# Two layers of sliding attention and SiLU feed-forward on one Trainium2 core: the second layer's first feed-forward product by Strassen's scheme

## The chip, the cores and the metric

The kernel runs on one core of one Trainium2 chip. The metric is the device time of one execution in microseconds. Three runs of the kernel before took 2225.85, 2226.11 and 2229.71 us; the median is 2226.11 us.

## What is computed

Two layers with the same weights, each an attention over eight earlier positions two apart, and a feed-forward block; 2048 tokens of width D = 576, 32 heads, F = 4608.

```
x = x + attention(layernorm(x), wqkv, wo)     # 32 heads of 18, window 8, dilation 2, softmax
x = x + silu(layernorm(x) @ w1) @ w2          # w1 is 576 x 4608, w2 is 4608 x 576
x = x + attention(layernorm(x), wqkv, wo)
x = x + silu(layernorm(x) @ w1) @ w2
```

Inputs and output are float32. TensorE (PE) is fed float16: each operand is split into a high half and a low half (the rest after rounding), and a product is the sum of high x high, high x low and low x high.

## The kernel before

**Tiling.** The tokens go in four chunks of 512 (NJ = 4 blocks of 128), once per layer: stages s = 0 to 3 are the first layer, s = 4 to 7 the second; below they are called chunks 0 to 7. F is cut into 36 tiles of 128. Per chunk and tile f, `ffn` has 14 matmuls of 512 columns for the first product (L861, weights of w1 stationary, the chunk's normalised activations `xb` moving, into the PSUM bank `z`), a SiLU on ScalarE (L863, `hs` from `z`), the high half of h on ScalarE (L865) and its low half on VectorE (L868). The 14 passes cover K = 576 as four blocks of 128 with three passes each and a block of 64 that holds both halves. After a group of tiles (G1 = 9), the second product has, per token block j and tile, six matmuls of 288 columns (L882, h stationary, w2 moving, into `acc`), and VectorE adds the group's sum to x (L743). Chunk 0 makes the float16 halves of w1 and w2 (`raw_split`) and GpSimd (POOL) stores them in DRAM; later chunks load them back through SyncE's queue, 320 KB of w1 and 288 KB of w2 for a tile (`load_w1`, `load_w2`).

**Around it.** `front(s)` makes the chunk's inputs: layer norm, q, k, v (L566, 432 columns; for chunks 1 to 3 they are made ahead, in the first stage), the attention on VectorE (L664 to L705), the projection (L736) and the layer norm ahead of the feed-forward block. In the second layer `front(s+1)` runs on the other engines while PE is in chunk s. Operands are turned by DMA transposes on SyncE's queue (L361).

**What sets the order.** Every operation is a record with an engine, an assumed duration, a priority and the buffers it needs (`op`). `Plan.order` plays the program through with these durations and writes each engine's instructions in the order in which they would start; so each engine's order is fixed when the program is built, and an engine waits at an instruction whose inputs are late. A tag is a set of buffers of one kind (`z` has 2, `hs` 3, `h` 10, `w1` 6, `w2` 11); a buffer is taken when the first operation that needs it starts, and is free again after the last.

```
pp, pd = s + 0.5, s - 0.5          # PE of chunk s; its loads, SiLU and additions
op("PE", 3.05, mm, [(xT, j) for j in range(NJ)] + ka, [z], pp)
op("ACT", 0.7, ..., [z, ("s12", f)], [hs], pd, table="silu")
```

A front has priority s - 1.0, so on PE the q, k, v of chunk s + 1 go ahead of what is left of chunk s. Lower numbers go first.

Of the kernel before, what the change touches and what calls it, by code (L numbers as in the profile page):

```python
# [11 lines left out]
I32 = mybir.dt.int32  # L12
# [24 lines left out]
HSH = 2.0 ** -5  # L37

# [12 lines left out]
class Plan:  # L51
# [10 lines left out]
    def slots(self, tag, tiles, turns):  # L62

        self.tags[tag] = tiles
        self.turns[tag] = 0 if turns else None
        self.named[tag] = 0
# [35 lines left out]
    def order(self):  # L102
# [9 lines left out]
        times = [0.0]  # L112

# [53 lines left out]
        while done < len(self.ops):  # L167
# [9 lines left out]
            while events and events[0][0] <= now:  # L177
                _, _, b = heapq.heappop(events)
                free[b.tag].append(b.slot)
            for e in engines:  # L180
# [7 lines left out]
                while ready[e]:  # L188
# [5 lines left out]
                    if all(len(free[t]) - want.get(t, 0) >= c for t, c in n.items()) and all(  # L194
                            self.turns[b.tag] in (None, b.turn) for b in need):
                        o = x[2]
                        break
# [7 lines left out]
                for b in o.bufs:  # L205
                    if b.slot is None:
                        b.slot = free[b.tag].pop(0)
# [24 lines left out]
def sliding_attention_silu_ffn(ctx: ExitStack, tc: tile.TileContext, x, wqkv, wo, w1, w2, out):  # L232
# [17 lines left out]

    tag("x", 8, [P, D], F32)
    tag("xa", 1, [P, 9, TB], F16)
    tag("xb", 2, [P, 9, TB], F16)
    tag("wq", 2, [P, 10, 3 * UC], F16)
    tag("kv", 2, [P, NI, 2, UC], F32)
    tag("qt", 2, [P, NJ, UC], F32)
    tag("o", 1, [P, NJ, D], F32)
# [4 lines left out]
    tag("y", 2, [P, D], F32, turns=False)  # L262
    tag("yh", 2, [P, 9, P], F16, turns=False)
    tag("oT", 2, [P, 9, P], F16, turns=False)
    tag("wo", 1, [P, 10, D], F16)
    tag("w1", 6, [P, 10, P], F16)
    tag("w2", 11, [P, 2, D], F16)
    tag("h", 10, [P, 2, TB], F16)
    tag("hs", 3, [P, TB], F32)
# [3 lines left out]
    tag("z", 2, [P, TB], F32, ps)  # L273
    tag("acc", 2, [P, 2, 512], F32, ps, turns=False)
    tag("misc", 2, [P, 512], F32, ps, turns=False)
# [3 lines left out]
    w2s = [tc.dram_tile([P, 2 * D], F16, name=f"w2s{f}") for f in range(NFT)]  # L279
    wqs = [tc.dram_tile([P, 30 * UC], F16, name=f"wqs{u}") for u in range(NU)]  # L280
# [35 lines left out]
    shs = [cp.tile([P, NFT], F32, name=f"sh{i}") for i in range(2)]  # L316
    d2s = [cp.tile([P, NFT], F32, name=f"d2{i}") for i in range(2)]
    pace = cp.tile([1, 1], F32, name="pace")
    cg = cp.tile([P, NFT], F32, name="cg")
# [50 lines left out]
    def layer_norm(xs, prio, into, on_act, on_pe=False):  # L370
# [28 lines left out]
        def newton():  # L399
            v, r, a, b = (T(nt)[:, i, :] for i in (0, 1, 3, 4))  # L400
            if on_act == 2:
                nc.vector.tensor_scalar(v, T(st)[:, :, 0, 1], 1.0 / D, EPS, op0=ALU.mult, op1=ALU.add)
            else:
                nc.vector.tensor_scalar(v, T(mv)[:, :, 1], EPS, None, op0=ALU.add)
            nc.vector.tensor_scalar(a.bitcast(I32), v.bitcast(I32), 1, None, op0=ALU.logical_shift_right)
            nc.vector.tensor_scalar(r.bitcast(I32), a.bitcast(I32), -1, 0x5F3759DF, op0=ALU.mult, op1=ALU.add)
            for s in (1.0, LNS):

                nc.vector.tensor_tensor(a, r, r, op=ALU.mult)
                nc.vector.tensor_tensor(a, a, v, op=ALU.mult)  # L410
                nc.vector.tensor_scalar(b, a, 0.375 * s, -1.25 * s, op0=ALU.mult, op1=ALU.add)
                nc.vector.tensor_tensor(b, b, a, op=ALU.mult)
                nc.vector.scalar_tensor_tensor(r, b, 1.875 * s, r, op0=ALU.add, op1=ALU.mult)
            if on_act in (1, 3):
                nc.vector.tensor_scalar(T(nt)[:, 2, :], T(mv)[:, :, 0], -1.0, None, op0=ALU.mult)
        op("DVE", 2.4, newton, [(st, j) for j in range(NJ)] + [(mv, j) for j in range(NJ) if on_act != 2], [nt], prio)
        for j in range(NJ):
# [20 lines left out]
            else:  # L438
                op("DVE", 0.6, norm, [xs[j], (mv, j), nt], [y, (xT, "hold")], prio)
# [70 lines left out]
    def load_wq(u, prio):  # L510
        w = Unit("wq")
        op("SP", 0.4, lambda: nc.sync.dma_start(fl(T(w.bufs[0])), wqs[u]), [("wqs", u)], w.keys, prio, nbytes=P * 20 * QR)
        return w
# [83 lines left out]
    def attention(s, xT, wq, more=None):  # L597
# [4 lines left out]
        for u in range(NU):  # L602
# [11 lines left out]
            else:  # L614
# [13 lines left out]
                for j in range(NJ):  # L628
                    m = Buf("misc")

                    def evac(j=j, m=m, u=u, kv=kv, qt=qt):
# [5 lines left out]
                       [(xT, j)] + w.keys, [m], pr_)  # L637
# [113 lines left out]
    def load_w2(f, prio):  # L751
        w = Buf("w2")
# [24 lines left out]
    def raw_split(f0, prio):  # L777
# [11 lines left out]
        for f in fs:  # L789
# [6 lines left out]
        op("PE", 0.3, lambda: nc.tensor.matmul(T(m)[:, :2 * n], ones, fl(accw[:, sl, :]), start=True, stop=True),  # L796
           [("accw", f, i) for f in fs for i in range(2)], [m], prio - 1)
# [23 lines left out]
    def group_scale(i, g, n):  # L821

        sl = slice(g * n, (g + 1) * n)
# [7 lines left out]
        op("DVE", 0.7, fn, [("s12", f) for f in range(g * n, (g + 1) * n)], [("sh", i, g), ("cg", g)], -0.5)  # L831

    def ffn(s, xT, xs):
# [3 lines left out]
        lay, c = divmod(s, NC)  # L837
        for g in range(NFT // n):
            hb, wbs = [], []
            if raw:  # L840
# [5 lines left out]
                group_scale(0, g, n)  # L846
# [24 lines left out]
            for j in range(NJ):  # L871
# [3 lines left out]
                last = s == NL * NC - 1 and j == NJ - 1 and g == NFT // n - 1  # L875
                for hs_ in ((0,), (1,)) if last else ((0, 1),):
                    for t in range(0, n, step):
                        def mm2(j=j, acc=acc, t=t, step=step, hb=hb, wbs=wbs, hs_=hs_):
                            for q in range(t, t + step):
                                for m, (a, w) in enumerate(((0, 0), (0, 1), (1, 0))):  # L880
                                    for h in hs_:
                                        nc.tensor.matmul(T(acc)[:, h, 0:288], T(hb[q])[:, a, j * P:(j + 1) * P],  # L882
                                                         T(wbs[q][0])[:, w, h * 288:(h + 1) * 288],
                                                         start=q == 0 and m == 0, stop=q == n - 1 and m == 2)
                        op("PE", 0.37 * step * len(hs_), mm2, [(hb[q], a) for q in range(t, t + step) for a in range(2)]
                           + [k for q in range(t, t + step) for k in wbs[q][1]], [(acc, h) for h in hs_], pp)
                    if last:
                        h, = hs_

                        def add_half(j=j, acc=acc, g=g, h=h):  # L890
                            x_ = T(xs[j])[:, h * 288:(h + 1) * 288]
                            nc.vector.scalar_tensor_tensor(x_, T(acc)[:, h, 0:288], d2s[i][:, g:g + 1], x_,
                                                           op0=ALU.mult, op1=ALU.add)
                        op("DVE", 0.45, add_half, [(acc, h), ("sh", i, g), xs[j]], [(xs[j], h)], pd)
# [100 lines left out]
```

## Time and profile before

| | us |
|---|---|
| runs (three) | 2225.85, 2226.11, 2229.71 |
| profiled execution, first to last instruction | 2229.8 |
| PE busy | 2180.4 (98%) |
| VectorE (DVE) busy | 1393.3 (62%) |
| ScalarE (ACT) busy | 747.4 (34%) |
| POOL busy | 206.3 (9%) |

The profiled execution is one execution; its span is as long as the slowest of the three runs. In the profile's rows, PE is the matmul itself, PEld the load of its stationary operand; L861 is line 861. The row of a group gives its busy time, the mean of one instruction in ns, and the idle time ahead of it with what ended it. Matmuls are pipelined: the mean of one contains the filling of the pipe, so the pace of a run of them is read from the start of a run to the start of the next.

### The profile page before, as it was taken

Reading aid. Unit: us, or ns where it says so; the run is one execution under the profiler, and the core shown is the slowest. Engines: PE = TensorE matmul, PEld = TensorE weight load, DVE = VectorE, ACT = ScalarE, POOL = GpSimd, SP = SyncE. Lnnn points to the kernel's source line nnn. Section 1 sums busy time; section 2 is a strip of 40 time slices with the busy share of each in tenths; the row PEclk is TensorE's granted clock in tenths of the full one; section 3 lists DMA queues with packets and bytes.
Section 4 is the critical chain, followed back from the end, with each engine's and each line's share of the span. In section 5 each row is a group of like instructions: output and inputs, shape, how many; then the busy total and the mean of one; then the engine's idle time right before and its main releaser. Section 6 shows DMA issues by size and latency. Waiting matters only on the chain.

```text
span 2229.8 us, 33919 instructions
## 1 busy us (share of the span) xinstructions
PE 2180.4 (98%) x13858; PEld 1350.7 (61%) x13858; DVE 1393.3 (62%) x2047; ACT 747.4 (34%) x1211; POOL 206.3 (9%) x341
## 2 busy tenths in 40 slices
PE   5999999999999999999999999999999999999999
PEld 3556565656666666655666656666666566666665
DVE  7999989889988311359834597336971389511111
ACT  6455777543132122224212232222322223222222
POOL 2133555200001000000000000000000000000000
PEclk9999999999999999999999999999999999999999
DMA  5577667784645433455445454454453643433331
GB/s 152 165 206 274 235 224 240 200 231 155 184 152 154 116 103 105 150 128 178 116 112 160 103 176 121 125 159 131 135 132 120 167 140 117 91 115 123 112 113 40
DMA packets 220564, 332.18 MB, mean 149 GB/s; under 512 B 107240, under 2 KB 127572, under 8 KB 216440
## 3 DMA queue, kind: packets, MB, share of 16 engines
q1 hardware_dynamic: 191408, 230.47, 36.4%
q0 software_dynamic: 20704, 78.02, 10.3%
q10 hardware_dynamic: 8296, 21.52, 3.5%
q8 instruction: 108, 1.77, 0.3%
q14 instruction: 48, 0.39, 0.1%
HBM read 240.08 MB, written 47.03 MB: 129 GB/s over the span
## 4 chain that ended last, share of the span: by engine, by line
PE 85%; DVE 6%; DMA 4%; issue 2%; ACT 1%; POOL 1%; ACTq 0%; SPq 0%; DVEq 0%; POOLq 0%
PE z L861 36%; PE acc L882 34%; PE misc L566 7%; PE acc L736 4%; PE z L566 3%; DMA w<-in_B_w_dram 1%; DVE pr L664 1%; DMA kv<-kv 1%; DVE pr L697 1%; DVE lg L668 1%; DMA oT<-yh 1%; DMA h<-in_A_wqkv_dram 1%; DVE x L743 0%; DVE w L807 0%; DVE pr L704 0%
## 5 line engine op out<-in xcount | busy, mean ns | idle before, releaser
L861 PE MATMUL z<-xb,w 128*128 128x512 f16 x4032 | 882.8, 380 | 7.9 <-issue 3.9
L882 PE MATMUL acc<-w,h 128*128 128x288 f16 x6912 | 856.1, 286 | 2.2 <-DVE h L868 1.3
L882 PEld LDWEIGHTS <-h 128*128 128x128 f16 x6912 | 676.4, 98 | 179.9 <-DVE h L868 1.6
L861 PEld LDWEIGHTS <-w 128*128 128x128 f16 x4032 | 394.8, 98 | 475.7 <-issue 6.7
L863 ACT ACTIVATE hs<-z,d 128x512 f32<-128x512 f32 x288 | 197.6, 686 | 979.9 <-PE z L861 962.2
L868 DVE SCALAR_TENSOR_TENSOR h<-hs,sh,h 128x512 f16<-128x512 f32 x288 | 213.8, 748 | 311.7 <-ACT h L865 311.6
L743 DVE SCALAR_TENSOR_TENSOR x<-acc,d,x 128x576 f32<-128x576 f32 x135 | 109.9, 814 | 325.1 <-PE acc L882 325.0
L664 DVE TENSOR_TENSOR pr<-qt,kv 128x2304 f32<-128x2304 f32 x64 | 163.3, 2551 | 89.3 <-DMA kv<-kv 66.4
L865 ACT ACTIVATE h<-hs,sh 128x512 f16<-128x512 f32 x288 | 207.5, 721 | 9.4 <-DVE d L830 0.3
L566 PEld LDWEIGHTS <-xa 128*128 128x128 f16 x1344 | 131.7, 98 | 121.2 <-issue 7.1
L566 PE MATMUL misc<-wq,xa 128*128 128x432 f16 x1008 | 190.0, 349 | 3.8 <-ACT xa L359 2.5
L697 DVE TENSOR_TENSOR pr<-kv,pe 128x1152 f32<-128x1152 f32 x128 | 169.0, 1352 | 1.2
L668 DVE TENSOR_REDUCE lg<-pr 128x128 f32<-128x2304 f32 x64 | 163.1, 2548 | 1.2
L704 DVE TENSOR_TENSOR pr<-pr 128x1152 f32<-128x1152 f32 (+1 forms) x128 | 135.1, 1056 | 3.5
L736 PE MATMUL acc<-wo,oT 128*128 128x288 f16 x896 | 114.8, 288 | 4.6 <-DMA oT<-yh 4.6
L736 PEld LDWEIGHTS <-oT 128*128 128x128 f16 x896 | 88.3, 99 | 30.1 <-DMA oT<-yh 4.9
L633 ACT ACTIVATE kv<-misc,du 128x288 f32<-128x288 f32 x80 | 40.0, 500 | 138.5 <-PE misc L566 79.6
L906 POOL DMA_DIRECT2D out_dram<-x x12 | 6.5, 546 | 698.3 <-DVE x L743 698.3
L687 ACT ACTIVATE pe<-lg 128x256 f32<-128x256 f32 x32 | 13.3, 416 | 169.2 <-DVE lg L678 161.3
L566 PEld LDWEIGHTS <-xb 128*128 128x128 f16 x448 | 43.7, 98 | 38.6 <-ACT xb L359 0.9
L384 DVE BATCH_NORM_STATS2 st<-x 128x6 f32<-128x288 f32 x128 | 52.0, 448 | 10.9 <-DMA x<-in_A_x_dram 5.9
L743 DVE SCALAR_TENSOR_TENSOR x<-acc,so,x 128x576 f32<-128x576 f32 x32 | 26.1, 815 | 29.5 <-PE acc L736 29.4
(121 smaller groups left out, 1127.4 us busy)
## 6 DMA issues: line engine op xcount, KB each, us to landing
w<-w1s SPq DMA_DIRECT2D x252, 320.0 KB
w<-w2s SPq DMA_DIRECT2D x252, 288.0 KB
wq<-wqs SPq DMA_DIRECT2D x17, 1080.0 KB
kv<-kd POOLq DMA_DIRECT2D x8, 1584.0 KB, 8.2
w1s<-w POOLq DMA_DIRECT2D x36, 320.0 KB, 4.2
w<-in_B_w_dram POOLq DMA_DIRECT2D x36, 288.0 KB, 5.3
w2s<-w POOLq DMA_DIRECT2D x36, 288.0 KB, 4.2
kv<-kv ACTq DMA_DIRECT2D x20, 504.0 KB
```

Of the source, the lines that this page charges most:

```text
L566: nc.tensor.matmul(T(m)[:, :3 * UC], a, b, start=n == 0, stop=n == len(pl) - 1)
L664: nc.vector.tensor_tensor(T(pr), T(qt)[:, j:j + 2, None, :].to_broadcast([P, 2, W, UC]), win(T(kv), j, 2), op=ALU.mult)
L668: nc.vector.tensor_reduce(T(lg)[:, j:j + 2].rearrange("p a w h -> p (a w h)"), T(pr).rearrange("p a w (h d) -> p (a w h) d", d=DH), axis=A ...
L697: nc.vector.tensor_tensor(T(pr)[:, a].rearrange("p w (h d) -> p w h d", d=DH), v, T(pe)[:, j + a, :, :, None].to_broadcast([P, W, UH, DH]) ...
L704: nc.vector.tensor_tensor(t[:, :, 0:h, :], t[:, :, 0:h, :], t[:, :, h:2 * h, :], op=ALU.add)
L736: nc.tensor.matmul(T(acc)[:, h, 0:288], a, b[:, h * 288:(h + 1) * 288], start=n == 0, stop=n == len(pl) - 1)
L743: nc.vector.scalar_tensor_tensor(t, T(acc)[:, :, 0:288], d, t, op0=ALU.mult, op1=ALU.add)
L861: nc.tensor.matmul(T(z), v, u, start=m == 0, stop=m == len(pl) - 1)
L863: op("ACT", 0.7, lambda z=z, hs=hs, f=f: nc.scalar.activation(T(hs), T(z), AF.Silu, scale=d1[:, f:f + 1]), [z, ("s12", f)], [hs], pd, tabl ...
L865: op("ACT", 0.72, lambda hs=hs, h=h, f=f: nc.scalar.activation(T(h)[:, 0, :], T(hs), AF.Copy, scale=shs[i][:, f:f + 1]), [hs, ("sh", i, g) ...
L868: op("DVE", 0.75, lambda hs=hs, h=h, f=f: nc.vector.scalar_tensor_tensor(T(h)[:, 1, :], T(hs), shs[i][:, f:f + 1], T(h)[:, 0, :], op0=ALU. ...
L882: nc.tensor.matmul(T(acc)[:, h, 0:288], T(hb[q])[:, a, j * P:(j + 1) * P], T(wbs[q][0])[:, w, h * 288:(h + 1) * 288], start=q == 0 and m = ...
```

## The change

**Seven products for eight.** Two tiles of F make a pair (18 pairs, `NP`). The token blocks of a chunk are taken as two halves (blocks 0, 1 and blocks 2, 3), K = 576 as two halves of 288, and the pair's 256 columns as two tiles: a 2 x 2 by 2 x 2 block product, done with seven block products P1 to P7 in place of eight. Each block product has a weight form of 288 x 128 and an activation form of 288 x 256 (256 tokens). A form is stored in five blocks of 128 rows (`KB`): two high, one that holds both halves of the last 32 rows, two low; the product is seven matmuls of 256 columns.

```
def product(k, z, first, last, wf=wf):
    def mm():
        t, w, v = T(z)[:, 0:2 * P], T(wf[k]), T(xf[k])
        pl = ((0, 0), (3, 0), (0, 3), (1, 1), (4, 1), (1, 4), (2, 2))
        for m, (u, r) in enumerate(pl):
            nc.tensor.matmul(t, w[:, u, :], v[:, r, :], start=first and m == 0, stop=m == 6, skip_group_check=True)
    op("PE", 0.78, mm, [wf[k], (xf[k], 0), (xf[k], 1)], [z], pp)
```

In `ffn_pairs` the sums of the scheme are made partly in PSUM, partly in SBUF: products are added into three banks c, a, b, and between them a bank is copied out by ScalarE (`snap`, L1045) or added to a copy by VectorE (`add`, L1048).

```
product("P5", c, True, False)
product("P1", a, True, False)
snap(c, 3)
snap(a, 0)
product("P3", c, False, True)
product("P6", a, False, False)
product("P2", b, True, True)
snap(a, 1)
add(b, 0)
add(c, 1)
product("P7", a, False, False)
add(a, 3)
product("P4", a, False, True)
```

Then come three SiLUs on ScalarE (L1064, L1066, L1068), the high half of h for the pair (L1071, 1024 columns) and the low half (L1074 on VectorE). The second product (`second`, L1095) has the same matmuls as before; groups are 5, 4, 5 and 4 pairs (`G2`).

**Weight forms (`prepare`).** While the first layer runs, at priority `PREP` = 2.6, each pair's raw w1 is loaded once more by POOL (4 + 8 DMAs, L936 and L939), VectorE makes four sums (L947, 384 columns each), ScalarE the high halves (L955) and VectorE the low halves (L962) of seven forms, and POOL stores them (`wfs`, 1120 KB a pair, L967). The second layer loads a form of 160 KB for each product (`load_wf`, L972).

**Activation forms (`forms`).** In place of the second layer's layer norm into `xb`, VectorE normalises into `ya`, `yb` and makes eight differences; each of the seven forms is split by ScalarE and VectorE in two parts and turned by two DMA transposes.

**Buffers.** Many tags now share memory (`area`, `part`, and `places`, which the planner keeps apart): the weight forms lie in w1's place, the prepared forms in those of `wq` and `xa`, the activation forms (nine buffers `xf`, seven in use by a chunk) in that of `xb`, `ya` in that of the attention's output. In the second layer `z` and `misc` are four banks for products and for q, k, v alike, one buffer is left for a quarter of wqkv (`wz`), and the first layer norm of chunk 4 and these loads wait until the last pair's forms are stored:

```
+    def load_wq(u, prio, kind="wq"):
+        w = Unit(kind)
+        wait = [("wfs", NP - 1)] if kind == "wz" else []
...
-            o = attention(s, layer_norm(X[s], s - 1.0, "xa", False), lambda u: load_wq(u, s - 1.0))
+            o = attention(s, layer_norm(X[s], s - 1.0, "xa", False, late=[("wfs", NP - 1)]), lambda u: load_wq(u, s - 1.0, "wz"))
...
-        XT[s] = layer_norm(X[s], s - 1.0, "xb", s == 1, s == 0)
+        XT[s] = layer_norm(X[s], s - 1.0, "xb", s == 1, s == 0) if s < NC else forms(X[s], s - 1.0)
...
-        ffn(s, XT[s], X[s])
+        (ffn if s < NC else ffn_pairs)(s, XT[s], X[s])
+        if s == 0:
+            for q in range(NP):
+                prepare(q, PREP)
```

The scales of a pair's two tiles have to be equal, so the small matmul that sums squares in `raw_split` (18 calls) gets a second one that adds the neighbour's:

```
-        op("PE", 0.3, lambda: nc.tensor.matmul(T(m)[:, :2 * n], ones, fl(accw[:, sl, :]), start=True, stop=True),
...
+            nc.tensor.matmul(out, ones, v, start=True, stop=False)
+            nc.tensor.matmul(out, ones, turned, start=False, stop=True)
```

**How instructions stand, VectorE in chunk 4.** Before, in the feed-forward block of the second layer, while the next chunk's attention runs (L664, L668), VectorE's order has the low halves of h (L868) between the long operations:

```order
L868 SCALAR_TENSOR_TENSOR h4_118<-hs2_126,sh1_281,h4_118 128x512
L868 SCALAR_TENSOR_TENSOR h5_119<-hs1_125,sh1_281,h5_119 128x512
L664 TENSOR_TENSOR pr0_87<-qt0_81,kv0_79 128x2304
L868 SCALAR_TENSOR_TENSOR h6_120<-hs0_124,sh1_281,h6_120 128x512
L668 TENSOR_REDUCE lg0_84<-pr0_87 128x128
```

In the change the same place (pairs 11 to 13 of chunk 4; L744 and L748 are the attention's lines there) reads, with the banks z0, z1, misc0 and misc1:

```order
L1048 TENSOR_TENSOR wq_69<-z0_101,wq_69 128x256
L1048 TENSOR_TENSOR wq_69<-misc1_104,wq_69 128x256
L748 TENSOR_REDUCE lg0_86<-pr0_89 128x128
L1048 TENSOR_TENSOR wq_69<-misc0_103,wq_69 128x256
L1048 TENSOR_TENSOR hs_72<-misc1_104,hs_72 128x256
L1074 SCALAR_TENSOR_TENSOR h_71<-wq_69,sh2_268,h_71 128x1024
L1048 TENSOR_TENSOR hs_72<-z0_101,hs_72 128x256
L744 TENSOR_TENSOR pr0_89<-qt1_85,kv1_83 128x2304
L1048 TENSOR_TENSOR hs_72<-z1_102,hs_72 128x256
```

VectorE now reads PSUM banks that PE needs again, three times a pair, between the same long operations. On PE the products of these pairs stand so (one row of each product's seven matmuls; the bank tells the product: pair 12's P5, P1, then P2, P3, P6, then pair 11's last):

```order
L1041 MATMUL z0_101<-xb_67,w1_70 128x256
...
L1041 MATMUL z1_102<-xb_67,w1_70 128x256
...
L1041 MATMUL misc1_104<-xb_67,w1_70 128x256
...
L1041 MATMUL z0_101<-xb_67,w1_70 128x256
...
L1041 MATMUL z1_102<-xb_67,w1_70 128x256
...
L1041 MATMUL misc0_103<-xb_67,w1_70 128x256
```

Between two products into the same bank that need a copy in between, two others stand here (P1 and P2 between P5 and P3 in z0). Over the second layer's 343 waits of a product for ScalarE or VectorE, one product stands between in 14 cases; in the others there are at least two products, or a piece of twelve second-product matmuls.

**POOL in the first layer.** The weight forms' loads and stores stand alone in POOL's order from chunk 2 to the last quarter of chunk 3's first products; two pairs of them:

```order
L967 DMA wfs9_206<-xa_66 128x4480
L936 DMA wq_69<-in_B_w1_dram 128x2x128 x4
L939 DMA wq_69<-in_B_w1_dram 32x2x128 x8
L967 DMA wfs10_207<-xa_66 128x4480
L936 DMA wq_69<-in_B_w1_dram 128x2x128 x4
```

The store of a pair stands behind the twelve loads for the pair after next. ScalarE's high halves of a pair (L955) wait for the store of the pair before, as the forms have one buffer (`wg`); the loads wait for the pair's first low halves (L962). Between the store of pair 10 and that of pair 17 the program has 264 matmuls of 512 columns and 580 of 288 on PE.

**PE at the end of chunk 3.** Before, the projection for chunk 4 (L736) ends with 140 first-product matmuls (512 columns) and 432 second-product matmuls (288 columns) of chunk 3 still to come. In the change it ends here (L816), and behind it stand 28 and 216 of them; then come the first products of chunk 4:

```order
L816 MATMUL acc1_106<-wo0_93,yo_73 128x288
...
L1137 MATMUL z0_101<-xb_67,w1_70 128x512
...
L1156 MATMUL acc0_105<-w2_94,h_71 128x288
...
L1156 MATMUL acc1_106<-w2_94,h_71 128x288
...
L1041 MATMUL z0_101<-xb_67,w1_70 128x256
```

The front of chunk 4 has moved later against PE's work: its first q, k, v matmul stood behind 116 of the first layer's 144 tiles of the first product, and now stands behind 122.

More of the change, by code (lines that the diff above doesn't have):

```diff
@@ L37 @@
 HSH = 2.0 ** -5
+NP = NFT // 2
+KH = D // 2
+KB = 5 * P
+LNX = 512.0
+G2 = (5, 4, 5, 4)
+W2N = 11
+PREP = 2.6
 class Buf:
@@ L112, in order, with open_slots @@
         times = [0.0]
+        taken = {}
+        def open_slots(t):
+            return [i for i in free[t] if not any(
+                lo < b and a < hi for n, lo, hi in self.places[t][i] for a, b in taken.get(n, ()))]
         def arrive(o):
@@ L873, in ffn @@
                 step = n if n < 6 else 3
[L875 to L894, printed above, removed]
```

333 lines of the change are left out of this document (278 added, 55 removed).

## The prediction

> **What bounds the kernel now.** The page comes first: PE is busy 98% of the span, and the chain that ended last is 85% PE. So time is what PE's instructions take, unless a change makes PE wait.
>
> ```profile
> PE 2180.4 (98%) x13858; PEld 1350.7 (61%) x13858; DVE 1393.3 (62%) x2047; ACT 747.4 (34%) x1211; POOL 206.3 (9%) x341
> PE 85%; DVE 6%; DMA 4%; issue 2%; ACT 1%; POOL 1%; ACTq 0%; SPq 0%; DVEq 0%; POOLq 0%
> ```
>
> Next come the windows. The second row is one chunk of the second layer (chunk 4 into 5): columns are length, then busy time of PE, PEld, DVE, ACT, POOL, then clock, DMA share, GB/s.
>
> ```profile
> 300.00:350.00 50.00, 47.68 (x292) 28.34 (x291) 43.60 (x76) 36.54 (x68) 27.29 (x48) 1.00 0.66 224
> 1350.70:1620.35 269.65, 269.37 (x1707) 166.68 (x1705) 165.20 (x228) 71.90 (x114) 2.21 (x4) 1.00 0.48 137
> ```
>
> PE has 0.28 us idle in 269.65, so in the second layer there is no wait to remove: a gain can come only from fewer or shorter PE instructions. PE's timeline of that chunk gives their pace (start, length, instruction, count; a run's time goes to the next run's start).
>
> ```profile
> 1350.69 21.32 PE L861 MATMUL z<-xb,w 128*128 128x512 f16 x98
> 1371.84 7.02 PE L736 MATMUL acc<-wo,oT 128*128 128x288 f16 x56
> ...
> 1381.72 7.02 PE L736 MATMUL acc<-wo,oT 128*128 128x288 f16 x56
> 1388.58 3.18 PE L861 MATMUL z<-xb,w 128*128 128x512 f16 x14
> 1391.60 26.62 PE L882 MATMUL acc<-w,h 128*128 128x288 f16 x216
> 1418.06 27.36 PE L861 MATMUL z<-xb,w 128*128 128x512 f16 x126
> 1445.26 26.62 PE L882 MATMUL acc<-w,h 128*128 128x288 f16 x216
> 1471.72 24.34 PE L861 MATMUL z<-xb,w 128*128 128x512 f16 x112
> 1495.89 18.05 PE L566 MATMUL misc<-wq,xa 128*128 128x432 f16 x98
> 1513.78 3.19 PE L861 MATMUL z<-xb,w 128*128 128x512 f16 x14
> ...
> 38.01 0.67 PE L357 MATMUL acc<-ident,yh 128*128 128x128 f16 x9
> L357 PE MATMUL acc<-ident,yh x180: 216/219/314, 16.1 to 221.2; 128*128 128x128 f16 x180
> ```
>
> 512 columns: 27.20 / 126 = 0.2159 us. 432: 17.89 / 98 = 0.1825. 288: 26.46 / 216 = 0.1225. The last two rows are of chunk 0's transposes of 128 columns, each with a stationary load of its own: nine took 0.67 us, less the 0.219 that one lasts (the middle of the three durations), over 8, is 0.056 us. The four lie on a line, 0.417 ns a column and some 2.5 ns each, so 256 columns take 0.1092 us (an estimate).
>
> **The change: what it removes.** Per chunk of the second layer, 36 x 14 = 504 matmuls x 0.2159 = 108.8 us go, and 18 x 49 = 882 x 0.1092 = 96.3 us come. That is -12.5 us a chunk, **-50.0 us** for four. The bounds: at the pace of 288 columns the gain is 0.8 us a chunk, 3 in all (rival C); below 0.1092 nothing speaks for it. The second product keeps its matmuls.
>
> Added on PE: the second small matmul in `raw_split`, 18 times.
>
> ```profile
> 345.07 0.28 PE L796 MATMUL misc<-accw,ones 128*128 128x4 f32 x2
> 345.21 0.38 PE L861 MATMUL z<-xb,w 128*128 128x512 f16 x1
> ```
>
> The call that is there (two records) delays the next matmul by 0.14 us and lasts 0.28: +2.5 to +5 us; I take **+2.5**, the delay. Chunk 0's order of PE changes in places too; its idle time there (2.3 us in the first of the two windows) is at stake both ways, which I carry as 0 ± 5.
>
> **What it adds beside PE, and what of it PE waits for.** Products are half as long as a tile before (0.76 for 3.02 us), and PE now waits for copies out of its banks.
>
> ```profile
> L868 DVE SCALAR_TENSOR_TENSOR h<-hs,sh,h 128x512 f16<-128x512 f32 x288 | 213.8, 748 | 311.7 <-ACT h L865 311.6
> L664 DVE TENSOR_TENSOR pr<-qt,kv 128x2304 f32<-128x2304 f32 x64 | 163.3, 2551 | 89.3 <-DMA kv<-kv 66.4 <-ACT kv L633 21.9
> L865 ACT ACTIVATE h<-hs,sh 128x512 f16<-128x512 f32 x288 | 207.5, 721 | 9.4 <-DVE d L830 0.3
> L863 ACT ACTIVATE hs<-z,d 128x512 f32<-128x512 f32 x288 | 197.6, 686 | 979.9 <-PE z L861 962.2 <-DMA kv<-kv 10.8 <-DVE lg L668 5.5
> L805 ACT ACTIVATE w<-w,s 128x640 f16<-128x640 f32 x36 | 29.3, 818 | 11.9 <-PE z L861 10.8 <-DVE s L330 1.0
> L807 DVE SCALAR_TENSOR_TENSOR w<-w,s,w 128x640 f16<-128x640 f32 x36 | 31.4, 877 | 0.0
> L678 DVE TENSOR_TENSOR lg<-lg,mx 128x256 f32<-128x256 f32 x32 | 13.6, 425 | 1.1
> 1543.93 0.50 ACT L633 ACTIVATE kv<-misc,du 128x288 f32<-128x288 f32 x1 [10.34 <-DVE pr L697]
> 1544.33 0.38 ACT L635 ACTIVATE qt<-misc,du 128x144 f32<-128x144 f32 x1
> 1544.75 7.46 PE L566 MATMUL misc<-wq,xa 128*128 128x432 f16 x40 [0.28 <-ACT qt L635]
> 1547.50 0.50 ACT L633 ACTIVATE kv<-misc,du 128x288 f32<-128x288 f32 x1 [2.14 <-PE misc L566]
> ```
>
> Loads: a copy of 256 columns out of PSUM takes 0.47 us on ACT (between the 0.38 and 0.50 of 144 and 288), an addition 0.43 on DVE. For 1024 columns: ACT 0.721 + 512 x 0.76 ns (818 less 721 over 128) = 1.11; DVE 0.748 + 512 x 1.01 ns = 1.26. A pair then costs ACT 4 x 0.47 (three copies, one SiLU) + 0.69 + 0.42 + 1.11 = 4.1 us, before 2 x 1.41 = 2.8; DVE 3 x 0.43 + 1.26 = 2.5, before 1.5. Per chunk that is +23 us on ACT and +19 on DVE, and `forms` adds, by the same slopes, some 10 on ACT (14 parts) and 7 on DVE: ACT 106 and DVE 191 us of a chunk of 257. Neither is full; only the moments count.
>
> The shortest hand-over: the run at 1544.75 ends its first 14 matmuls at 1547.30 (14 x 0.1825), ACT starts at 1547.50, and after ACT's end at 1544.71 PE starts at 1544.75. So product, copy, next product costs 0.20 + 0.47 + 0.04 = 0.71 us, less than the one product of 0.76 that stands between in the tightest 14 places; elsewhere there is 1.47 or more. PE waits where a copy is queued behind something longer than planned: an addition (L1048) behind a 2.55 us attention operation comes 0.20 + 2.55 + 0.43 = 3.2 us after its product, 1.7 late against 1.5 of cover. There are 16 such operations in each of three chunks; the planner gave them 2.57 us and 0.45 to 0.48 to the copies, so its own places hold. Bounds 0 and 48 x 1.7 = 82 us; near the first, since no assumed duration is short: I take 3 late ones, **+5**.
>
> **The preparation** costs a pair on DVE four sums of 384 columns at 0.55 and low halves of 2688 columns in four operations, 2.72 + 4 x 0.23, together 5.8; on ACT 2.04 + 4 x 0.33 = 3.4; on POOL 13 DMAs. That is 105 us of DVE, 61 of ACT and 234 DMAs. It lies beside chunks 1 to 3, where DVE has time. But its chain may set PE's pace, since copies and low halves of chunk 3 are queued behind L955 and L962 on engines that keep their order.
>
> ```profile
> L770 POOL DMA_DIRECT2D w<-in_B_w_dram x36 | 27.5, 764 | 14.7 <-issue 6.2 <-DMA kd<-w 4.8 <-PE z L861 1.8
> L772 POOL DMA_DIRECT2D w<-in_B_w_dram x72 | 38.4, 537 | 5.5 <-DMA w<-in_B_w_dram 3.0 <-issue 1.3 <-PE z L861 1.1
> w<-in_B_w_dram POOLq DMA_DIRECT2D x36, 256.0 KB, 5.0
> wqs<-wq POOLq DMA_DIRECT2D x2, 1080.0 KB, 8.1
> wqs<-wo POOLq DMA_DIRECT2D x1, 1080.0 KB, 5.4
> wqs<-h POOLq DMA_DIRECT2D x5, 216.0 KB, 9.9
> ```
>
> A round of it: ACT's first high half 1.11, DVE's low half 1.26, twelve loads issued 4 x 0.54 to 0.76 + 8 x 0.54 = 6.5 to 7.4, the store's issue 0.54 and its landing 5.4 to 8.1 (1120 KB, nearest the 1080 KB rows): 14.8 to 18.4 us. PE's work between two stores is 264 x 0.2159 + 580 x 0.1225 = 128.0 over 7 = 18.3 us. So it holds, barely at the upper end. With a microsecond of queueing the upper end is 19.4, over by 1.1 x 12 late pairs = 13 us. Bounds 0 and 13, above that rival B; I take **+3**.
>
> **The ends of chunks.** Behind the projection for chunk 4 PE now has 28 x 0.2159 + 216 x 0.1225 = 32.5 us (before: 140 and 432 matmuls, 83 us).
>
> ```profile
> 1363.40 3.25 SPq L361 DMA_TRANSPOSE oT<-yh  x2
> ...
> 1375.46 4.70 SPq L361 DMA_TRANSPOSE oT<-yh  x2
> ...
> 1395.83 7.72 SPq L361 DMA_TRANSPOSE xb<-yh  x4
> ```
>
> From the projection's last matmul (1388.58) to the first transpose took 7.3 us. `forms` has three more normalisations and eight differences before it, some 5 us: 12; a copy and a low half add 1.3. A transpose of 1152 columns takes SyncE 1.6 us (3.25 / 2; the new ones have 640), and PE could use two that ended at 1380.16 from 1381.72. So the first form is there at 12 + 1.3 + 3.2 + 1.6 = 18 us, and the last of the seven, fourteen transposes on, at 37 at the latest, when PE after 32.5 us has six products ahead of it. Bounds 0 and 10; **+2**. At the three later ends, five of the seven forms wait for chunk s's last pair to free its buffers, under 192 x 0.1225 = 23.5 us of second product; ten transposes take at most 16 and the wait after them: 0 to 3 each, **+3** together. Loads of weight forms are 1120 KB a pair for 640 before, +8.8 MB or 34 GB/s in a chunk; with 137 x 269.65 / 257 = 144 that is 178 GB/s, under the 224 of the first window: 0.
>
> **Sum.** -50.0 + 2.5 + 5 + 3 + 2 + 3 = -34.5. The profiled execution, 2229.8 us, is as long as the slowest run, with nothing around its span; the median is 3.7 lower. 2229.8 - 34.5 - 3.7 = **2191.6**.
>
> **The rivals.**
> A: *copies bind.* If all of ACT's 106 us a chunk fell into the 96.3 us of products, PE would wait 9.7 a chunk, 39 for 5: 2226, no change. For it: one ACT order for copies, SiLU, q, k, v and halos. Against: a third of PE's chunk is second product, which the planner uses as filler. 0.07.
> B: *the preparation paces the first layer.* If each of the twelve loads waits for one issued eight earlier to land (5.0 us: 10 us a round) and the store lands in 9.9 as the wqs<-h row did, a round is 1.11 + 1.26 + 10 + 0.54 + 9.9 = 22.8, 4.5 over 18.3; x 17 = 77 in place of 3: 2266, **slower**. It decides from 18.3 + 37.5/17 = 20.5 us a round. For it: one buffer of forms. Against: the rows above. 0.10.
> C: *the stationary load shows.* If a 256-column matmul cannot hide the next load, it takes the 0.1225 of 288 columns: 47 us of the gain gone, 2238, slower. Against: 0.056 us at 128 columns with loads. 0.03.
> The Trainium skill ("TensorE: Matmul & The Clock Gate", Back-to-back issue gap) says that a stream of load and matmul pairs runs at about 81 ns with 128 columns against 56 for an isolated gap; by that, as an estimate, 256 columns would take 25 ns more, 118 us a chunk, and the kernel 2280. By that rule the change loses; the trace's 56 ns, with a load for each transpose, does not agree, and its chance is in C's.
>
> **How the numbers follow.** The forecast has 0.80; A 0.07, B 0.10, C 0.03. A measurement tells 0.2%, 4.5 us, from no change. Faster: 0.80 + 0.02 of A = 0.82; same: 0.04 of A; slower: B, C and 0.01 of A = 0.14. Range: low, all waits 0 and chunk 0 luckier by 5: 2229.8 - 50 + 2.5 - 5 - 3.7 = 2174. High: the waits at 18 (copies), 13, 8, the small matmul 5: -50 + 44 = -6, 2220, and a little of A: 2222. Outside are B, C, 0.05 of A and 0.02 below, 0.20 in all.
>
> **What would show it.** Right: L1041's 3528 matmuls at 0.109 us, a chunk of the second layer in about 259 us, PE's idle time there under 5 a chunk. For A: waits of PE for ACT and DVE (L1045, L1048) of ten or more a chunk. For B: the first layer from 560 to 1120 us longer, POOL or ACT's L955 waiting for the store. For C: PE's busy time in L1041 over 400 us. A wait at L646 in chunk 3 or a gap at the first L1041 would be the ends of chunks. Wrong would be above all a chain of the preparation that is longer than its rows.

## The result and the profile after

| | before | after |
|---|---|---|
| median of four runs, us | 2226.24 | 2207.53 |
| lowest to highest, us | 2225.85 to 2229.71 | 2206.12 to 2214.10 |
| profiled execution, span, us | 2229.8 | 2206.6 |

The ratio is 0.9917, 95% interval 0.9901 to 0.9933: faster by 18.7 us, where 34.5 were forecast. The gain is real, about half its size is missing, and the profile says where. The page of the changed kernel, its first line and its chain:

```profile
PE 2139.0 (97%) x15406; PEld 1503.4 (68%) x15406; DVE 1578.4 (72%) x2453; ACT 905.3 (41%) x1617; POOL 347.2 (16%) x575
PE 90%; DMA 5%; DVE 2%; ACT 1%; issue 1%; ACTq 0%; POOL 0%; SPq 0%; DVEq 0%; POOLq 0%
```

PE is still the bound, but its share fell from 98% to 97% while its work shrank. The windows of the changed kernel (columns as in the prediction) show where it idles:

```profile
560.00:790.00 230.00, 230.00 (x1538) 150.19 (x1536) 215.13 (x301) 77.92 (x103) 51.92 (x85) 1.00 0.63 189
790.00:1020.00 230.00, 230.00 (x1449) 141.45 (x1447) 109.98 (x180) 87.30 (x124) 68.70 (x118) 1.00 0.67 211
1250.00:1350.00 100.00, 94.39 (x672) 66.36 (x671) 70.62 (x70) 34.07 (x68) 5.81 (x8) 0.97 0.55 157
1610.00:1870.00 260.00, 252.66 (x2030) 198.93 (x2029) 181.40 (x283) 96.89 (x194) 2.16 (x4) 0.99 0.65 177
```

While the preparation runs (first and second row) PE has no idle time at all. In the second layer, where PE had 0.28 us idle in 269.65 before, it now misses 5.61 us in one stretch and 7.34 in another, and in both the granted clock is below 1. The waits of PE from 1120 us on, in full (engine, tile and line, what it waited for, total, times, longest):

```profile
PE z L1041 <- ACT hs L1045: 7.2, 1, 7.2
PE misc L1041 <- ACT hs L1064: 5.6, 1, 5.6
PE misc L1041 <- ACT wq L1045: 2.7, 1, 2.7
PE acc L1095 <- DVE x L1104: 0.6, 1, 0.6
```

Three waits, 15.5 us, all for ScalarE (two copies out of a bank, L1045, and a SiLU, L1064, that also reads a bank), one in each of chunks 4, 5 and 6. PE's timeline at the first, and at a quiet place (the first two rows of the fence):

```profile
1421.97 1.69 PE L1041 MATMUL z<-xb,w 128*128 128x256 f16 x14
1423.50 0.93 PE L1041 MATMUL misc<-xb,w 128*128 128x256 f16 x7
...
1309.21 1.63 PE L1095 MATMUL acc<-w,h 128*128 128x288 f16 x12
1316.46 1.65 PE L1041 MATMUL misc<-xb,w 128*128 128x256 f16 x7 [5.61 <-ACT hs L1064]
1317.90 1.70 PE L1041 MATMUL z<-xb,w 128*128 128x256 f16 x7
1319.39 1.35 PE L1041 MATMUL misc<-xb,w 128*128 128x256 f16 x7
1320.58 0.93 PE L1041 MATMUL z<-xb,w 128*128 128x256 f16 x7
```

The quiet place gives the pace: 1.53 / 14 = 0.1093 us for 256 columns, as forecast. After the wait seven matmuls take 1.44, 1.49 and 1.19 us instead of 0.76, until the clock is back, so the 5.61 us cost 7.4. ScalarE's timeline at the same place tells why the SiLU was late; the last three rows are an ordinary set of the same instruction, and the same place one and two chunks on:

```profile
1305.99 0.37 ACT L715 ACTIVATE qt<-misc,du 128x144 f32<-128x144 f32 x1
1306.12 9.77 ACTq L725 DMA_DIRECT2D kv<-kv  x4
1315.93 0.47 ACT L1064 ACTIVATE hs<-misc,accw 128x256 f32<-128x256 f32 x1 [9.57 <-DMA kv<-kv]
...
1279.38 2.89 ACTq L725 DMA_DIRECT2D kv<-kv  x4
...
1569.69 6.91 ACTq L725 DMA_DIRECT2D kv<-kv  x4
...
1824.38 10.55 ACTq L725 DMA_DIRECT2D kv<-kv  x4
```

L725 are the four halo DMAs of a unit (a quarter of the heads), issued from ScalarE's queue. Thirteen of the sixteen sets from 1000 us on take 2.87 to 3.46 us to issue, which is what the planner assumes (3.2). The third set that is issued while PE is in chunk 4, 5 and 6 (it belongs to the chunk after) takes 9.77, 6.91 and 10.55, and ScalarE's reading of the banks stands behind it. Before, the sixteen sets (L645) took 2.87 to 3.40; the one at the same place:

```profile
1280.93 3.10 ACTq L645 DMA_DIRECT2D kv<-kv  x4
```

SyncE's timeline in the changed kernel, same moment:

```profile
1305.58 0.32 SPq L592 DMA_DIRECT2D wq<-wqs  x1
1306.35 13.60 SPq L972 DMA_DIRECT2D w<-wfs  x7
```

SyncE begins a quarter of wqkv (1080 KB) and then seven weight forms. The single instructions of the trace give the semaphore that each DMA completes on (S, numbers of the trace; start in us):

```
SP   1305.58 wqkv quarter  S107      SP   1307.87 weight form 3  S105
ACT  1306.12 halo 1        S108      SP   1308.64 weight form 4  S106
SP   1306.35 weight form 1 S102      SP   1312.22 weight form 5  S107  (after the wqkv quarter landed)
ACT  1306.71 halo 2        S100      ACT  1315.07 halo 4         S108  (waits for S108: halo 1 landed)
SP   1307.11 weight form 2 S103      SP   1318.14 weight form 6  S100  (waits for S104, S100: halos 3 and 2)
ACT  1307.59 halo 3        S104
```

SyncE's and ScalarE's DMAs share eight semaphores (S100 and S102 to S108 in these traces; POOL's DMAs have S110 to S117), dealt out in the program's order; a DMA waits until the one that had its semaphore before has landed. With five weight forms dealt in between, halo 4 got halo 1's semaphore, and halo 1 took 8.9 us to land. The transfer was nearly as long before (7.9 us for halo 1 of the set at the same place); the wait for it is new. At the other two places the semaphore came from another DMA: in chunk 5 halo 4 got the semaphore of the wqkv quarter (S104), which landed at 1575.77, and halo 4 began at 1575.79; in chunk 6 it got that of halo 2 (S107), which landed at 1834.09, and began at 1834.11. That is theory L below.

To compare stages, take each matmul's time to the next one's start less the pace of its kind (0.2159, 0.1825, 0.1225, 0.1092, 0.056 us; the matmuls are 2164.0 us of it before and 2114.0 after) and add up what is left: idle time, slow clock, and the small matmuls. One profiled execution each, us:

| kernel | first 550 us | 550 to 1200 | from 1200 | span |
|---|---|---|---|---|
| before | 46.8 | 0.4 | 1.1 | 2229.8 |
| changed | 54.0 | -0.1 | 21.5 | 2206.6 |
| changed_again | 57.4 | -0.1 | 23.6 | 2211.6 |
| small_twice | 53.7 | 0.3 | 0.6 | 2235.8 |
| prep_only | 50.8 | -0.1 | 2.0 | 2231.1 |
| halo_pool | 54.6 | -0.1 | 6.3 | 2193.5 |
| wf_pool | 55.7 | -0.1 | 17.9 | 2204.0 |
| wq_pool | 53.0 | -0.1 | 27.0 | 2211.5 |
| halo_wq_pool | 46.4 | -0.1 | 8.3 | 2185.7 |
| pool_dve_sum | 49.4 | -0.1 | 10.4 | 2190.6 |
| halo_wq_pool_dve_sum | 50.3 | 2.1 | 18.5 | 2201.7 |
| halo_planned | 56.2 | -0.1 | 52.7 | 2240.3 |
| halo_pool_planned | 56.4 | -0.1 | 19.6 | 2206.9 |

So the change is -50.0 + 7.2 + 20.4 - 0.5 (550 to 1200) - 0.4 (PE's first matmul is earlier) = -23.3, the two spans' difference of 23.2. The span before is 3.6 above the median of the runs, the span after 0.9 below, which makes 18.7 of it.

Part of the first column is slow clock. From 31 to 550 us the clock is at half for 6.83 us in the kernel before and in halo_wq_pool, 13.65 in the changed kernel and pool_dve_sum, 20.48 in changed_again and halo_pool. Seven matmuls took 1.49 us for 0.76 in the slow stretch above, so at most half of that time is lost: up to 3.4 of the 7.2 us by which the changed kernel's chunk 0 is worse than before.

### The profile page after: what moved, and what is told of

It is laid out like the page before. It is cut to its first block, busy times and chain, and to the rows that moved or that the text cites. A ratio compares the mean times of both kernels' runs of the same rounds, so it can differ in the third digit from the quotient of the medians.

```text
span 2206.6 us, 39058 instructions
## 1 busy us (share of the span) xinstructions
PE 2139.0 (97%) x15406; PEld 1503.4 (68%) x15406; DVE 1578.4 (72%) x2453; ACT 905.3 (41%) x1617; POOL 347.2 (16%) x575
## 4 chain that ended last, share of the span: by engine, by line
PE 90%; DMA 5%; DVE 2%; ACT 1%; issue 1%; ACTq 0%; POOL 0%; SPq 0%; DVEq 0%; POOLq 0%
PE acc L1095 19%; PE acc L1156 19%; PE z L1137 18%; PE misc L1041 8%; PE z L1041 8%; PE z L646 7%; PE misc L646 6%; PE acc L816 5%; DMA kv<-kv 1%; DMA yo<-yh 1%; DMA h<-in_A_wqkv_dram 1%; DMA w1s<-w 1%; DMA w<-in_B_w_dram 1%; DVE pr L777 0%; DMA wq<-wqs 0%
## 5 line engine op out<-in xcount | busy, mean ns | idle before, releaser
L1137 PE MATMUL z<-xb,w 128*128 128x512 f16 x2016 | 443.9, 380 | 12.4 <-ACT hs L1139 5.2
L1095 PE MATMUL acc<-w,h 128*128 128x288 f16 x3456 | 439.2, 286 | 0.6 <-DVE x L1104 0.6
L1095 PEld LDWEIGHTS <-h 128*128 128x128 f16 x3456 | 338.0, 98 | 85.4 <-issue 0.8
L1041 PEld LDWEIGHTS <-w 128*128 128x128 f16 x3528 | 346.3, 98 | 62.6 <-issue 17.3
L1137 PEld LDWEIGHTS <-w 128*128 128x128 f16 x2016 | 197.0, 98 | 247.6 <-DVE w L892 8.2
L1041 PE MATMUL misc<-xb,w 128*128 128x256 f16 x1764 | 224.5, 274 | 8.5 <-ACT hs L1064 5.6
L1041 PE MATMUL z<-xb,w 128*128 128x256 f16 x1764 | 224.6, 274 | 7.5 <-ACT hs L1045 7.2
L1139 ACT ACTIVATE hs<-z,d 128x512 f32<-128x512 f32 x144 | 98.4, 683 | 298.1 <-PE z L1137 292.7
L744 DVE TENSOR_TENSOR pr<-qt,kv 128x2304 f32<-128x2304 f32 x64 | 163.4, 2554 | 14.3 <-DMA kv<-kv 10.4
L1144 DVE SCALAR_TENSOR_TENSOR h<-hs,sh,h 128x512 f16<-128x512 f32 x144 | 106.3, 747 | 90.0 <-ACT h L1141 89.8
L748 DVE TENSOR_REDUCE lg<-pr 128x128 f32<-128x2304 f32 x64 | 163.1, 2549 | 1.3
L816 PE MATMUL acc<-wo,yo 128*128 128x288 f16 x896 | 117.1, 291 | 8.0 <-DMA yo<-yh 7.8
L646 PE MATMUL misc<-wq,xa 128*128 128x432 f16 x574 | 112.5, 352 | 3.4 <-ACT xa L436 2.5
L646 PE MATMUL z<-wq,xa 128*128 128x432 f16 x602 | 114.4, 346 | 1.1 <-ACT hs L659 0.6
L816 PEld LDWEIGHTS <-yo 128*128 128x128 f16 x896 | 88.7, 99 | 33.6 <-DMA yo<-yh 8.1
```

What stands on the lines that cost most here:

```text
L646: nc.tensor.matmul(T(m)[:, :3 * UC], a, b, start=n == 0, stop=n == len(pl) - 1)
L744: nc.vector.tensor_tensor(T(pr), T(qt)[:, j:j + 2, None, :].to_broadcast([P, 2, W, UC]), win(T(kv), j, 2), op=ALU.mult)
L748: nc.vector.tensor_reduce(T(lg)[:, j:j + 2].rearrange("p a w h -> p (a w h)"), T(pr).rearrange("p a w (h d) -> p (a w h) d", d=DH), axis=A ...
L816: nc.tensor.matmul(T(acc)[:, h, 0:288], a, b[:, h * 288:(h + 1) * 288], start=n == 0, stop=n == len(pl) - 1)
L1041: nc.tensor.matmul(t, w[:, u, :], v[:, r, :], start=first and m == 0, stop=m == 6, skip_group_check=True)
L1095: nc.tensor.matmul(T(acc)[:, h, 0:288], T(hb[t])[:, a, f, j * P:(j + 1) * P], T(wbs[t][f])[:, w, h * 288:(h + 1) * 288], start=t == 0 and ...
```

## The experiments

**The halo DMAs on POOL (halo_pool).** In the changed kernel's order of every other engine:

```
-    nc.scalar.dma_start(t[p0 + d:p0 + d + n, i:i + m], t[p0:p0 + n, 11 - m:11])
+    (nc.gpsimd if lay else nc.scalar).dma_start(t[p0 + d:p0 + d + n, i:i + m], t[p0:p0 + n, 11 - m:11])
```

> The changed kernel with the four halo DMAs of each unit in the second layer issued by POOL instead of ACT; every other engine keeps its order. Theory L (shared semaphores): SP's and ACT's DMAs are dealt eight completion semaphores in program order; in the third halo of chunks 4, 5 and 6 so many loads come between that ACT's fourth halo DMA waits for the first to land, and ACT's copies out of the banks stand behind it. Then the three waits of PE (15.5 us) and the slow clock behind two of them (some 4) go: about 2187 us (2184 to 2190). Theory C (ACT is simply too full there: rival A of the prediction): ACT only loses the 2.9 us of issue per halo, PE still waits for L1045 and L1064, 2203 us or more.

Measured: 2195.28 us, ratio to the kernel before 0.9848 (0.9824 to 0.9871). PE's waits from 560 us on and one window, which is the stretch that had 94.39 of 100:

```profile
PE z L1041 <- DMA w<-wfs: 2.5, 1, 2.5
PE z L1041 <- DVE hs L1048: 1.0, 1, 1.0
PE z L1041 <- DMA xb<-yo: 0.6, 1, 0.6
PE acc L1095 <- DVE x L1104: 0.6, 1, 0.6
PE misc L1041 <- DMA w<-wfs: 0.3, 1, 0.3
```

```profile
1250.00:1350.00 100.00, 100.00 (x733) 71.44 (x731) 75.78 (x81) 37.23 (x72) 14.19 (x24) 1.00 0.60 171
```

The three waits are gone and what is lost from 1200 us on falls from 21.5 to 6.3. Theory C falls: ScalarE has the same copies and does not hold PE up. The time missed the forecast of 2187 by 8: a weight form is late next, 2.5 us, and this job's kernel before was 1.1 slower.

**The weight forms on POOL (wf_pool), the halos left on ScalarE.**

```
-    nc.sync.dma_start(fl(T(w)), wfs[q][:, i * KB:(i + 1) * KB])
+    nc.gpsimd.dma_start(fl(T(w)), wfs[q][:, i * KB:(i + 1) * KB])
```

> The changed kernel with the 504 loads of weight forms issued by POOL instead of SP; the halo DMAs stay on ACT, the same bytes move in the same order of each engine. Theory L: the loads take no semaphore of the eight that ACT's halo DMAs share, ACT's four halo issues take some 2.9 us everywhere, the three waits go: 2187 us (2184 to 2192, with POOL's 0.5 us an issue unseen). Theory B (the 1080 KB load of wqkv and the weight forms slow the halo's transfer): the bytes are the same, ACT's third halo still takes 7 us or more and PE waits: 2203 or more. Theory C (ACT too full): 2203 or more.

Measured: 2202.8 us, ratio 0.9885 (0.9862 to 0.9908). The third halo of chunk 4 and the SiLU behind it on ScalarE, then PE's two longest waits:

```profile
1312.91 3.18 ACTq L725 DMA_DIRECT2D kv<-kv  x4
1316.20 0.47 ACT L1064 ACTIVATE hs<-misc,accw 128x256 f32<-128x256 f32 x1 [3.05 <-PE misc L1041]
```

```profile
PE z L1041 <- DMA xb<-yo: 5.0, 1, 5.0
PE z L1041 <- DMA w<-wfs: 4.0, 2, 3.1
```

The bytes are the same, halo 1 takes 8.5 us to land (8.9 in the changed kernel), and yet the issue takes 3.18 us: it is the shared semaphores, not the bytes (theory B falls). The time itself missed: PE now waits for weight forms and for an activation form instead. Why these are late with the loads on POOL was not tried.

**Only the wqkv quarters on POOL (wq_pool, one run).**

```
-    nc.sync.dma_start(fl(T(w.bufs[0])), wqs[u])
+    (nc.gpsimd if wait else nc.sync).dma_start(fl(T(w.bufs[0])), wqs[u])
```

> The changed kernel with only the loads of wqkv in the second layer (1080 KB each, L592) on POOL in place of SP. They stand ahead of the first halo DMA, so they take none of the semaphores between the first and the fourth. Theory L: the waits stay, three of 2.5 to 7.5 us, 2203 to 2212 us. Theory Q (the big load ahead in SP's own queue is what holds things up): the waits go, 2187.

Measured: 2213.27 us, a microsecond above theory L's band. The third halo on ScalarE in chunk 4:

```profile
1311.60 10.31 ACTq L725 DMA_DIRECT2D kv<-kv  x4
1321.96 0.47 ACT L1064 ACTIVATE hs<-misc,accw 128x256 f32<-128x256 f32 x1 [10.11 <-DMA kv<-kv]
```

The long issue stays (10.31 here, 10.26 in chunk 6; in chunk 5 it went, and a second unit's set in chunk 4 took 9.24). The deal of the semaphores moves with each DMA that leaves the pair of queues: the new long set waits for S107, dealt to a load of w2 before. Theory Q falls as the cause of all three. For chunk 5 it is half right, and what was expected here was wrong: there halo 4 had the wqkv quarter's own semaphore, and without the quarter the set takes 3.15. What holds ScalarE up is whichever DMA had the semaphore, a big load or a halo.

**The preparation alone (prep_only).**

```
-    XT[s] = layer_norm(X[s], s - 1.0, "xb", s == 1, s == 0) if s < NC else forms(X[s], s - 1.0)
+    XT[s] = layer_norm(X[s], s - 1.0, "xb", s == 1, s == 0)
...
-    (ffn if s < NC else ffn_pairs)(s, XT[s], X[s])
+    ffn(s, XT[s], X[s])
```

> The changed kernel with the second layer's feed-forward block as in the first layer (products of 512 columns, layer norm into xb); the preparation of all 18 pairs stays in the first layer, its forms are stored and not read. So it computes with the old products. If the preparation costs PE nothing, it is the kernel before plus what chunk 0 lost (7 us: the second small matmul and the waits): 2229 to 2236 us, and no idle time of PE from 560 to 1200 us. If the preparation costs time that the trace hid, it is above 2238.

Measured: 2236.88 us, ratio 1.0038 (1.0028 to 1.0049). In this kernel the last 128 tokens are also stored ahead of their last sum, so from PE's last matmul to the end it has 2.1 us instead of 3.9. From 550 to 1200 us PE loses nothing: the preparation is free there, and what this kernel loses in its profile it loses in chunk 0 (50.8 against 46.8) and not where the forms are made. The median is a microsecond over the band, as this job's kernel before was over the earlier one, and the early store hides some 1.8 us more. The profiled execution, 2233.41 us, is the second shortest of the ten, so where the longer ones lost their time is not known, and a hidden cost of a few us is not excluded by the times alone.

**The kernel before with the small matmul twice (small_twice).**

```
+    def twice():
+        for k in range(2):
+            nc.tensor.matmul(T(m)[:, :2 * n], ones, fl(accw[:, sl, :]), start=True, stop=True)
-    op("PE", 0.3, lambda: nc.tensor.matmul(T(m)[:, :2 * n], ones, fl(accw[:, sl, :]), start=True, stop=True),
+    op("PE", 0.5, twice,
```

> The kernel before with the small matmul of raw_split made twice (the second repeats the first) and planned at 0.5 us as in the changed kernel. If the second one costs PE its time, 18 calls cost 18 x 0.23 = 4.2 us (0.49 to 0.58 us a call in the changed kernel's trace, 0.26 to 0.32 before); with chunk 0's order moved as well, 2 to 8 us over the kernel before, so a ratio of 1.001 to 1.0035. If it hides beside other work: no difference.

Measured: 2233.03 us, ratio 1.0033 (1.0021 to 1.0046), 7 us, at the upper end. Its first 550 us lose 53.7, as the changed kernel's 54.0: the second matmul and the order that follows from it are enough for a chunk 0 as dear as the changed kernel's. One profiled execution each says so; halo_wq_pool, with the changed kernel's chunk 0 on PE, lost 46.4 there, no more than the kernel before. In the changed kernel's trace a call now reads:

```profile
333.24 0.28 PE L880 MATMUL misc<-accw,ones 128*128 128x4 f32 x2
333.38 0.36 PE L881 MATMUL misc<-accw,ones 128*128 128x4 f32 x2
333.61 1.63 PE L1156 MATMUL acc<-w,h 128*128 128x288 f16 x12
```

0.37 us to the next matmul for 0.14 before: 18 x 0.23 = 4.2 us.

**The neighbour's squares added by VectorE (pool_dve_sum), on top of halo_pool.**

```
-    nc.tensor.matmul(out, ones, v, start=True, stop=False)
-    nc.tensor.matmul(out, ones, turned, start=False, stop=True)
...
+    nc.tensor.matmul(out, ones, both, start=True, stop=True)
+op("DVE", 0.1, lambda: nc.vector.tensor_tensor(accw[:, f0, :], accw[:, f0, :], accw[:, f0 + 1, :], op=ALU.add),
...
```

> The changed kernel with the halo DMAs of the second layer on POOL (as in halo_pool) and the neighbour's squares added by VectorE before the small matmul, so that PE has one small matmul a call again. If the second matmul costs 4.2 us and VectorE's addition of two columns hides: halo_pool less 4, about 2191 us (2185 to 2195). If VectorE's step makes the chain of raw_split longer by as much: 2195 or more.

Measured: 2195.72 us, ratio 0.9866 (0.9851 to 0.9881). Chunk 0 loses 5.2 us less than in halo_pool (up to 3.4 of it by 6.83 us less at half clock), and the second layer 4.1 more, by waits for weight forms of up to 2.8 us: the planner laid all that follows differently. No gain in all; the two intervals overlap.

**Telling the planner the long issue (halo_planned).**

```
-    op("ACT", 3.2, halo, own, ...
+    op("ACT", 10.5 if lay else 3.2, halo, own, ...
```

> The changed kernel, halo DMAs on ACT as in the change, but the planner is told that a halo's issue takes ACT 10.5 us in the second layer in place of 3.2. Theory L with the planner: the copies are late only because their places were chosen for 3.2 us; with 10.5 the planner lays second-product matmuls over the issue, PE's waits behind it go and the kernel takes 2188 to 2198 us. If no such filler is ready at these places, or if the loads gather behind the halo all the same: 2203 or more.

Measured: 2236.82 us, ratio 1.0049 (1.0030 to 1.0068), slower than before. Issues of 9.90, 10.54 and 9.92 us are still there, and PE waits behind one of them alone, 1.5 us (L1064 below); but the order that makes room for sixteen long issues brings the activation forms late:

```profile
PE z L1041 <- DMA xb<-yh: 19.4, 3, 10.7
PE misc L1041 <- ACT yh L1008: 5.7, 1, 5.7
PE z L1041 <- DMA xb<-yo: 3.2, 4, 1.0
...
PE z L1041 <- ACT wq L1064: 1.5, 1, 1.5
```

The theory's first half held but for that wait, its time did not.

**halo_pool with the planner informed (halo_pool_planned):** the line of halo_pool, and `op("POOL" if lay else "ACT", 3.2, halo, ...)`.

> As halo_pool, and the planner knows that the halo DMAs are POOL's, so it orders ACT, VectorE and PE anew. If what is left in halo_pool (5 us of PE's waits for loads and forms in the second layer) is the order's doing: 2188 to 2193 us. If it is the transfers' (a burst of the wqkv load, halo and weight forms): as halo_pool, 2193 to 2199.

Measured: 2205.55 us, ratio 0.9905 (0.9889 to 0.9921), a miss by both accounts. A new order of the same work lost 19.6 us from 1200 us on, 10.0 of it in five waits for weight forms. Between two orders of one plan lie 10 us here.

**Halos and wqkv quarters on POOL (halo_wq_pool), the same with VectorE's addition (halo_wq_pool_dve_sum), and the changed kernel beside them (changed_again).** The edits are those of halo_pool, wq_pool and pool_dve_sum together.

> The changed kernel with halo DMAs and the second layer's loads of wqkv both on POOL (every other engine in its order), so that SP's queue holds the loads of weight forms and of w2 alone. If what is left in halo_pool (PE waits of up to 2.5 us for weight forms) comes from the 1080 KB load ahead of them in SP's queue: these waits go too, 2186 to 2191 us. If it is the bytes of the burst, wherever they are queued: 2191 to 2198 us.

> As halo_wq_pool, with the neighbour's squares added by VectorE before the small matmul (as in pool_dve_sum). Chunk 0 saves what pool_dve_sum saved there by its trace, 5 us against halo_pool: 2181 to 2190 us if the loads no longer hold up PE, 2188 to 2195 if they do.

> The changed kernel as it is, beside the other two on one chip. Theory L: the halo DMAs of the third unit in chunks 4 to 6 take 6.5 us or more on ACT again, the others 3, and PE waits 12 to 20 us for L1045 and L1064 in all: 2203 to 2212 us.

Measured: 2189.86 us, ratio 0.9845 (0.9829 to 0.9860); 2204.06, ratio 0.9910 (0.9895 to 0.9924); 2214.33, ratio 0.9958 (0.9942 to 0.9974). The first is the best version, 24.5 us under the changed kernel in the same job; by their ratios it and halo_pool are equal. Its time lies in the first band for another reason: waits for weight forms of 1.9 and 1.4 us are still there and the second layer loses 8.3, so the quarter ahead in SyncE's queue was not what made them; its profiled chunk 0 lost 8 us less. The second is 9 us above its upper band: once more another order in the second layer (18.5 lost). The third has the same three places again, PE's timeline of two of them:

```profile
1319.41 1.65 PE L1041 MATMUL misc<-xb,w 128*128 128x256 f16 x7 [5.39 <-DMA kv<-kv]
...
1580.88 1.50 PE L1041 MATMUL misc<-xb,w 128*128 128x256 f16 x7 [2.46 <-ACT wq L1045]
```

Its halo issues took 9.65, 6.70 and 10.50 us there: the wait is built into the program. Its time is 2.3 us over its band and 7 us longer than in the first job, outside that interval; in the profiled executions 3.4 of it is chunk 0, whose loss runs from 46.4 to 57.4 in kernels that have the same chunk 0 on PE. Up to 6.8 of these 11.0 us are slow clock (20.48 us at half against 6.83); why it varies so was not tried.

## Why the prediction was right in sign and too good by half

- **The pace of 256 columns, -50.0: right.** 0.1093 us measured, -50.0 by the sums of the paces. Rival C, and the rule cited with it, did not come: PE is not held by the stationary loads.
- **The second small matmul, +2.5: 4.2** by the typical call, near the upper of its two ends. I took the delay of one call in the old trace; the second pair of records takes 0.23.
- **Chunk 0's order, 0 +- 5: some 3**, what is left of 7.2; up to 3.4 can be the clock, and it is within the spread of that stage.
- **Copies out of the banks, +5: 20. This is the mis-sized term**, and the place was another one. I looked for the long operation ahead of a copy on VectorE and found none that the planner had assumed too short; that held: in the changed kernel PE's trace has 136 matmuls of L1041 that wait for VectorE, and none shows idle time for an addition (L1048); in halo_pool one costs 1.0. The step that failed is "no assumed duration is short", for ScalarE's halo issue: 3.2 assumed, 6.91 to 10.55 at three places. The trace of before had it short everywhere, and I did not ask what the 504 new loads do to a queue beside theirs. The remark on the loads, "178 GB/s, under the 224 of the first window: 0", priced their bytes and not their number: SyncE had 72 loads for a chunk's weights before and has 162 now, on the semaphores that the halos use. halo_pool and wf_pool take them apart from two sides, and the three long issues are gone in both.
- **The preparation, +3: 0.** Stores are 27.8 us apart (from 512.2 to 985.5, 18 of them), so a round took longer than the 20.5 from which rival B was to decide, and PE did not wait once: the last form is stored 170 us before the first is loaded (1154). The picture of PE tied to the rhythm of the stores was wrong, B's condition with it; only ScalarE stood still for the one buffer, 47.1 us in all. The store's line by itself, and the group of ScalarE's first high half:

```profile
L967 POOL DMA_DIRECT2D wfs<-xa x18: 532/569/622, 512.2 to 985.5; - x18
```

```profile
L955 ACT ACTIVATE xa<-wq,accw 128x1024 f16<-128x1024 f32 x18 | 20.5, 1140 | 78.9 <-DMA wfs<-xa 47.1 <-DVE x L823 24.9 <-DVE wq L947 6.8
```

- **The ends of chunks, +5: 0** in the changed kernel. The cover is thin all the same: in wf_pool an activation form came 5.0 us late, in halo_planned 10.7.
- **Median against profile, -3.7: +0.9.** I read the span before as the time of an execution "with nothing around its span". The execution profiled after took 2208.64 us for a span of 2206.6, so 2.0 lie around it, and its span is 0.9 under the median. Of the 15.9 us between the 2191.6 forecast and the time measured, 4.6 are this term and 11.3 the change. The +3 and +5 that did not come hide 8 of what the copies cost: that the forecast lies no further off is luck.

Of the rivals, A names the right engine (ScalarE's one order for copies, SiLU, q, k, v and halos), with a sum of busy time where the cost is a wait for a transfer; halo_pool has the same copies and loses 6.3.

## What to carry to other kernels

Price a new stream of DMAs by its number as well as its bytes: ask which queues share its completion semaphores, and how many of its issues fall between two DMAs of another engine that must not wait. A DMA issue in the queue of an engine that others wait for can last as long as a transfer (9.77 us here), so issue it where nobody stands behind it. When an order is planned from assumed durations, an edit that changes one of them reorders everything after it, so to test one cause keep the order and move only that instruction.

## What the hardware showed that was not expected

A short pause of PE can cost a slow clock or not. In the changed kernel PE paused 5.61, 2.67 and 7.18 us: from within the first and the last the clock is at half for 6.83 us each, behind the middle one not at all. In changed_again a pause of 2.46 us at nearly the same place was followed by 3.41 us at half clock, seen in the 1.50 us of its row above and in this window:

```profile
1570.00:1600.00 30.00, 27.54 (x219) 21.93 (x217) 21.77 (x27) 15.15 (x27) 0.00 (x0) 0.94 0.62 176
```

In halo_pool a pause of 2.52 us was not; in halo_pool_planned one of 2.17 was, and 21 matmuls behind it lasted 4.13 us in place of some 2.46:

```profile
1836.32 4.13 PE L1041 MATMUL z<-xb,w 128*128 128x256 f16 x21 [2.17 <-DMA w<-wfs]
```

In all these executions the slow stretches of the second layer are whole multiples of 3.41 us. The Trainium skill ("TensorE: Matmul & The Clock Gate", Part 1: The HAM clock gate) describes a window of 3413 ns that runs freely and so meets a pause at any phase; by that, the trace agrees. Its section on HAM oscillation asks for no idle gap over about 3.4 us; here 2.46 and 2.17 were enough to lose the clock, so the measurement decides for a smaller bound.
